# Weight-quarter sums by accumulating DMAs, token sums in six VectorE operations, output scaling on ScalarE, in an attention and top-1 expert kernel

## The chip, the cores and the metric

The kernel runs on one core of one Trainium2 chip. The metric is the device time in microseconds (us) of a whole execution. In the profile PE is TensorE, PEld its weight loads, DVE VectorE, ACT ScalarE, POOL GpSimd and SP SyncE; SPq and POOLq are the sequencers that issue DMAs.

## The reference

Attention with a linear bias over a window of 128 positions, then a layer of eight experts in which each token goes to one:

```python
x = attn_out.transpose(0, 2, 1, 3).reshape(4608, 512)     # attention, 8 x 8 heads, 576 positions
logits = xn @ en.T / tau
expert_idx = np.argmax(logits, axis=1)
gate_w = softmax(logits)[token, expert_idx]
for e in range(8):
    mask = expert_idx == e
    h = np.maximum(x[mask] @ w1[e], 0.0)                  # w1[e]: 512 x 1024
    out[mask] = gate_w[mask, None] * (h @ w2[e])          # w2[e]: 1024 x 512
```

All of it is float32. The kernel holds each factor as a high and a low float16 part and multiplies high by high, high by low and low by high.

## The kernel before

The first 300 us compute attention and the routing; tokens are scattered by expert into a DRAM buffer `xs`. The part that the change touches is `moe`, from about 270 us on. The experts are taken one after another as slots, each with a capacity in tokens (`SLOTS`, 512 to 688), in the order `TURNS` = 0, 1, 4, 3, 5, 6, 2, 7. Slots 0 and 1 (`PLAIN` = 2) use plain matmuls (`hidden`). The other six use a seven-product scheme for the first matmul: tokens are split into even and odd (halves of h columns, h = 256 to 312), the 512 inputs and the 1024 hidden units into halves, so that w1 has four quarters, named here 11, 12, 21, 22, and seven products of sums replace eight products of quarters (`seven`, the table `SEVEN`).

Stages of a slot s on PE: the **sevens** (four column groups `ft`, each seven steps of six matmuls, L1526), then the **output** (4 or 5 blocks of 128 tokens, 24 matmuls each with 512 columns, L1601; after slots 4 and 6 also one block `ps_t` that packs leftover tokens of several slots). While PE computes the output of one slot, the next slot is made ready:

- SP fetches w1 and w2 in pieces of 512 KB into a ring of `WSTG` = 6 staging tiles `ws` (`fetch`, L1397, L1399). A piece waits until the tile's former user is done.
- POOL makes the weight differences `tt`, `tu` from the w1 pieces (`differ`, L1431: eight per slot) and the token sums z1, z2, z4, z3 from the token tile `xT` (`x_sum`, L1451: ten per slot).
- ACT rounds every quarter, difference and sum to the high float16 part (L1414, L1461, for w2 L1483); DVE computes the low part from the same source and the high part (L1412, L1459, for w2 L1481). There is one pair of w1 part tiles, so these follow the sevens of the slot before.
- ACT or DVE in turn scales each output block by the gate (`scaled`, L1613, L1615) and POOL writes it to DRAM by token index (`put`, an indirect DMA, L440).
- DVE makes the row numbers `ids` and gates `gs` of the next slot (`row_info`, L1385 to L1388). These sit between the second and the third combining operation of the current slot's first column group; `ids` has two buffers, so the new one waits until the last `put` of the slot before the current one has landed.

In the sevens, ACT copies product a out of PSUM (`s`, L1539), DVE makes u2, u3 and the four quarters of the hidden layer from it (`combine`, L1537), ACT and DVE split these (`quarter`, L1559, L1557). Step 5 of a column group (ps7a again) waits for `s`, step 6 (ps7d) for u3, step 7 (ps7c) for the combining operation of ps7b.

A planner written in the kernel (`Plan.run`) sets the order: every operation is a job with an engine, an assumed duration, what it follows, what buffers it takes and a due time; each engine's instructions are then emitted in the order found. Engines work in order, so an instruction that waits holds up what is behind it.

Of the kernel before, what the change touches and what calls it, by code (L numbers as in the profile page):

```python
# [23 lines left out]
P = 128  # L24
# [12 lines left out]
WSTG = 6  # L37
# [164 lines left out]
def kernel(  # L202
# [1100 lines left out]
    def moe(mctx):  # L1303
        def pool(nm, n):
            return mctx.enter_context(tc.tile_pool(name=nm, bufs=n))

        xt, yp, st, ht, wT, wS, tp, zp = (
            pool(*a)
            for a in (("xt", 2), ("yp", 3), ("wstage", WSTG), ("ht", 1), ("wthird", 1), ("wseven", 1), ("wdiff", TBUFS), ("xsum", 1))
        )  # L1310
        MB = (MAXCAP + P - 1) // P
        MH = max(SLOTS[1:]) // 2
# [14 lines left out]
        def expert_of(s):  # L1327
            if s == 0:
                state[s] = dict(e=head_box["e"], w1=(w["w1h"], w["w1l"]), w2=(w["w2h"], w["w2l"]))
            else:  # L1330
                state[s] = dict(e=nc.sync.value_load(ebi[0:1, s : s + 1], min_val=0, max_val=E - 1))

# [71 lines left out]
        def split(s, what, c, lo):  # L1404

            if "w1" not in state[s]:
                state[s]["w1"] = [wS.tile([P, 2, 7, HF], F16, tag=f"w1{n}", name=f"w1{n}_{s}") for n in "hl"]
            i0, n = PIECES[what]
            x = {"a": ws[s, 1, c][:, 0:HF], "b": ws[s, 1, c + 2]}[what] if what in "ab" else ws[s, what, c].rearrange("p a f -> p (a f)")
            hi, lo_ = (a[:, c, i0 : i0 + n, :].rearrange("p a f -> p (a f)") for a in state[s]["w1"])  # L1410
            if lo:
                nc.vector.scalar_tensor_tensor(lo_, x, SW, hi, op0=ALU.mult, op1=ALU.subtract)  # L1412
            else:
                nc.scalar.activation(hi, x, AF.Copy, scale=SW)  # L1414

        def differ(s, i, c):

            what = "tu"[i // 2]
            if i % 2 == 0:
                ws[s, what, c] = tp.tile([P, 2, HF], F32, tag="tt", name=f"t{what}_{s}_{c}")  # L1420
            up, dn, o = ws[s, 1, c], ws[s, 1, c + 2], ws[s, what, c][:, i % 2, :]
            b11, b12, b21, b22 = up[:, 0:HF], up[:, HF:F], dn[:, 0:HF], dn[:, HF:F]
            if i == 0:
                a, b = b12, b11
            elif i == 1:
                a, b = b22, ws[s, "t", c][:, 0, :]
            elif i == 2:
                a, b = b22, b12
            else:
                a, b = b21, ws[s, "t", c][:, 1, :]  # L1430
            nc.gpsimd.tensor_tensor(o, a, b, op=ALU.subtract)  # L1431
# [3 lines left out]
        def x_sum(s, i, k):  # L1435

            h, xx = SLOTS[s] // 2, state[s]["xT"]
            a = {(t, d): [xx[:, b + 2 * d : b + 2 * d + 2, t : 2 * h : 2] for b in (0, KT)] for t in range(2) for d in range(2)}
            if k == 0:
                zs[s, i] = zp.tile([P, 2, MH], F32, tag="z", name=f"z{i}_{s}", bufs=ZBUFS)[:, :, 0:h]  # L1440
            z = zs[s, i]
            add, sub = ALU.add, ALU.subtract
            if i == 1:
                x, y, op = [(a[1, 0][0], a[1, 1][0], add), (z, a[1, 0][1], add), (z, a[1, 1][1], add)][k]
            elif i == 2:
                x, y, op = [(zs[s, 1], a[0, 0][0], sub), (z, a[0, 0][1], sub)][k]
            elif i == 3:
                x, y, op = [(a[0, 0][0], a[1, 0][0], sub), (z, a[0, 0][1], add), (z, a[1, 0][1], sub)][k]
            else:
                x, y, op = [(a[0, 1][0], zs[s, 2], sub), (z, a[0, 1][1], add)][k]  # L1450
            nc.gpsimd.tensor_tensor(z, x, y, op=op)  # L1451

        def x_split(s, i, lo):
            h = SLOTS[s] // 2
            if "S" not in state[s]:
                state[s]["S"] = zp.tile([P, 4, 2, 2, MH], F16, tag="S", name=f"S_{s}")
            hi, lo_ = (state[s]["S"][:, i - 1, b, :, 0:h] for b in range(2))
            if lo:
                nc.vector.tensor_tensor(lo_, zs[s, i], hi, op=ALU.subtract)  # L1459
            else:  # L1460
                nc.scalar.activation(hi, zs[s, i], AF.Copy)  # L1461

        def part(p, s, w, c, lo):
            if w == 1:
                if "w1" not in state[s]:
                    state[s]["w1"] = [
                        wS.tile([P, 2, 7, HF], F16, tag=f"w1{n}", name=f"w1{n}_{s}").rearrange("p a b f -> p (a b f)")[:, 0 : KT * F].rearrange("p (a f) -> p a f", f=F)
                        for n in "hl"
                    ]
# [42 lines left out]
        def seven(s, ft, n):  # L1512
# [12 lines left out]
            for m, (a, b, c) in enumerate(jobs):  # L1525
                nc.tensor.matmul(  # L1526
                    ps, a[:, c, idx, fs], b[:, c, :], start=(n in OPENS and m == 0), stop=(m == len(jobs) - 1), skip_group_check=True
# [6 lines left out]
        def combine(s, ft, what):  # L1534
            h = SLOTS[s] // 2
            b = {k: wb[s, ft, k][:, 0:h] for k in "abcd" if (s, ft, k) in wb}
            add = lambda o, x, y: nc.vector.tensor_tensor(o, x, y, op=ALU.add)  # L1537
            if what == "s1":
# [5 lines left out]
            elif what == "c22":  # L1544
                add(b["b"], b["c"], su[s, ft, "u3"])
            else:
                o = b["d" if what == "c21" else "c"]
                add(o, o, su[s, ft, "u2"])
# [77 lines left out]
        plan.caps.update(pt=8, ws=WSTG, xT=2, info=2, rows=2, h=1, y=3, w10=1, w1s=1, w20=1, w21=1, w22=1, tt=TBUFS, z=ZBUFS, S=1, s1=1, u2=2, u3=1)  # L1626
# [20 lines left out]
        for p, s in enumerate(TURNS):  # L1647
# [17 lines left out]
            if p:  # L1665
                last_ = TURNS[p - 1]
                m = starts[last_] + 24 * (0.42 * SLOTS[last_] + 5) * (3.5 if p > PLAIN else 4 if p > 1 else 2)
                for w_ in (1, 2):
                    for c in range(4):
                        d = (lead if w_ == 1 else m) + 1500 * c + 500  # L1670
                        a = (p, s, w_, c)
                        J(
                            f"get{w_}_{s}_{c}", "SP", 640, lambda a=a: fetch(*a), land=1800, moves=1400, makes=[("ws", ("ws",) + a)],
                            due=d - 3000 * (w_ == 1), after=before(f"expert{s}") + before(f"rows{last_}") + ([(f"get{w_}_{s}_{c-1}", ORDER)] if c else []),
                        )
                for c in range(2 if p >= PLAIN else 0):
                    up, dn = ("ws", p, s, 1, c), ("ws", p, s, 1, c + 2)
                    for i in range(4):
                        tk = ("tt", s, "tu"[i // 2], c)
                        J(  # L1680
                            f"dif_{s}_{c}_{i}", "POOL", 1130, lambda a=(s, i, c): differ(*a), lock=(1130,),
                            after=[f"get1_{s}_{c}", f"get1_{s}_{c + 2}"] + ([f"dif_{s}_{c}_{i - 1}"] if i else []),
                            makes=[("tt", tk)] if i % 2 == 0 else [], uses=[tk, up, dn] + ([("tt", s, "t", c)] if i == 3 else []), due=lead + 4000 + 5000 * c + 1200 * i,
                        )
                    for n, what in enumerate("btua"):
                        src = {"a": [up], "b": [dn], "t": [("tt", s, "t", c)], "u": [("tt", s, "u", c)]}[what]
                        dep = {"a": [f"get1_{s}_{c}"], "b": [f"get1_{s}_{c + 2}"], "t": [f"dif_{s}_{c}_1"], "u": [f"dif_{s}_{c}_3"]}[what]
                        half = what == "a"
# [249 lines left out]
```

## Time and profile before

| | us |
|---|---|
| median of 3 runs | 704.51 (701.58 to 704.75) |
| the profiled execution, its time | 699.6 |
| its span, first to last instruction | 697.9 |
| PE / DVE / ACT / POOL busy | 600.5 / 544.2 / 374.8 / 436.3 |

The span is 1.7 us under the profiled execution's own time, and that is 4.9 us under the median. Busy shares are means over the span; attention and the expert layer differ, so the views below are read by stretch. A row of a timeline gives start, duration, engine, line, operation, output<-input, and in brackets how long the engine had been idle and what released it.

### The profile page before, as it was taken

Reading aid. Unit: us, or ns where it says so; the run is one execution under the profiler, and the core shown is the slowest. Engines: PE = TensorE matmul, PEld = TensorE weight load, DVE = VectorE, ACT = ScalarE, POOL = GpSimd, SP = SyncE. Lnnn points to the kernel's source line nnn. Section 1 sums busy time; section 2 is a strip of 40 time slices with the busy share of each in tenths; the row PEclk is TensorE's granted clock in tenths of the full one; section 3 lists DMA queues with packets and bytes.
Section 4 is the critical chain, followed back from the end, with each engine's and each line's share of the span. In section 5 each row is a group of like instructions: output and inputs, shape, how many; then the busy total and the mean of one; then the engine's idle time right before and its main releaser. Section 6 shows DMA issues by size and latency. Waiting matters only on the chain. (4 is left out here: it accounts for less than half of the span.)

```text
span 697.9 us, 17376 instructions
## 1 busy us (share of the span) xinstructions
PE 600.5 (86%) x6613; PEld 402.7 (58%) x6613; DVE 544.2 (78%) x1203; ACT 374.8 (54%) x860; POOL 436.3 (63%) x563
## 2 busy tenths in 40 slices
PE   7999998999898899989939973992996797499996
PEld 5877777777766655556427442741744543264664
DVE  5987998999989991735926986796796798769680
ACT  6999897988879741622603622441461362235320
POOL 8878598789888872059680686098078368607301
PEclk9999999999999999999988995998899799599999
DMA  9999999999999777983630651173084055300101
GB/s 196 192 192 175 198 212 200 197 234 204 192 257 203 114 236 242 264 220 66 183 141 1 144 181 56 36 225 108 1 241 138 1 162 176 95 1 16 57 16 47
DMA packets 213589, 101.52 MB, mean 145 GB/s; under 512 B 195829, under 2 KB 195829, under 8 KB 213504
## 3 DMA queue, kind: packets, MB, share of 16 engines
q1 hardware_dynamic: 207664, 81.47, 56.6%
q0 software_dynamic: 5840, 18.92, 7.5%
q8 instruction: 53, 0.87, 0.5%
q14 instruction: 32, 0.26, 0.1%
HBM read 61.92 MB, written 19.70 MB: 117 GB/s over the span
## 5 line engine op out<-in xcount | busy, mean ns | idle before, releaser
L1526 PEld LDWEIGHTS <-w1h 128*128 128x128 f16 x672 | 68.6, 102 | 84.6 <-issue 63.9
L1601 PE MATMUL ps<-w2h,hl 128*128 128x512 f16 (+1 forms) x264 | 98.4, 373 | 0.6 <-DVE hl L1565 0.5
L1601 PE MATMUL ps<-w2h,hh 128*128 128x512 f16 (+1 forms) x264 | 98.4, 373 | 0.0
L1601 PE MATMUL ps<-w2l,hh 128*128 128x512 f16 (+1 forms) x264 | 98.4, 373 | 0.0
L688 ACT ACTIVATE pe<-sc,nm 128x128 f32<-128x128 f32 x288 | 85.0, 387 | 7.5 <-DVE rs L780 2.9
L1601 PEld LDWEIGHTS <-hh 128*128 128x128 f16 x528 | 51.5, 98 | 57.7 <-issue 0.8
L1451 POOL TENSOR_TENSOR z<-xT,z 128x528 f32<-128x528 f16 (+4 forms) x6 | 12.5, 2076 | 113.1 <-DVE S L1459 113.0
L440 POOL DMA_INDIRECT out_dram<-y,ids x32 | 41.8, 1306 | 56.6 <-DMA xs<-zrow 22.9
L1451 POOL TENSOR_TENSOR z<-z,xT 128x528 f32<-128x528 f32 (+4 forms) x42 | 70.3, 1675 | 2.1
L540 DVE SCALAR_TENSOR_TENSOR pq<-ptp,pq 128x512 f16<-128x512 f32 x72 | 53.0, 736 | 13.8 <-ACT pq L537 13.7
L1526 PE MATMUL ps7c<-S,w1h 128*128 128x264 f16 (+4 forms) x192 | 39.0, 297 | 25.9 <-DVE ps7b L1537 25.9
L537 ACT ACTIVATE pq<-ptp 128x512 f16<-128x512 f32 x72 | 55.2, 767 | 10.3 <-PE ptp L696 7.6
L1526 PE MATMUL ps7a<-xT,w1h 128*128 128x264 f16 (+4 forms) x192 | 40.9, 305 | 21.5 <-ACT s L1539 21.5
L1481 DVE SCALAR_TENSOR_TENSOR w2l<-ws,w2h 128x1024 f16<-128x1024 f32 x28 | 53.1, 1911 | 7.7 <-ACT w2h L1483 7.7
L696 PE MATMUL ptp<-ident,pe 128*128 128x128 f32 x288 | 48.0, 284 | 12.2 <-DVE pq L540 5.8
L1559 ACT ACTIVATE hh<-ps7b 128x264 f16<-128x264 f32 (+4 forms) x24 | 11.6, 484 | 86.8 <-DVE ps7b L1537 86.8
L664 PE MATMUL sc<-kh,qh 64*64 64x192 f32 (+3 forms) x1280 | 57.7, 288 | 0.0
L681 DVE TENSOR_REDUCE nm<-sc 128x2 f32<-128x256 f32 x144 | 55.7, 410 | 0.1
L664 PEld LDWEIGHTS sc<-kh,qh 64*64 64x64 f32 (+1 forms) x1280 | 44.6, 139 | 8.7 <-issue 3.5
L1483 ACT ACTIVATE w2h<-ws 128x1024 f16<-128x1024 f32 x28 | 28.8, 1050 | 37.6 <-DMA ws<-moe_w_dram 37.6
L813 POOL TENSOR_TENSOR gx<-xf,gx 128x512 f16<-128x512 f32 x36 | 42.2, 1173 | 8.5 <-DVE gx L802 6.0
L613 POOL TENSOR_TENSOR vo<-ldv,vh 128x512 f16<-128x512 f32 x36 | 40.7, 1135 | 6.7 <-ACT vh L605 6.2
(272 smaller groups left out, 1842.1 us busy)
## 6 DMA issues: line engine op xcount, KB each, us to landing
ws<-moe_w_dram SPq DMA_DIRECT2D x56, 512.0 KB, 4.8
ldk<-k_dram SPq DMA_DIRECT2D x32, 256.0 KB, 4.7
ldq<-q_dram SPq DMA_DIRECT2D x32, 256.0 KB, 4.9
ldv<-v_dram SPq DMA_DIRECT2D x32, 256.0 KB, 5.2
stg<-moe_w_dram SPq DMA_DIRECT2D x16, 256.0 KB, 4.0
ldk<-k_dram SPq DMA_DIRECT2D x8, 128.0 KB
ldq<-q_dram SPq DMA_DIRECT2D x8, 128.0 KB, 4.7
ldv<-v_dram SPq DMA_DIRECT2D x8, 128.0 KB, 5.3
```

What stands on the lines that cost most here:

```text
L440: ins = nc.gpsimd.indirect_dma_start(out[:, :], bass.IndirectOffsetOnAxis(ap=ids, axis=0), y, None, bounds_check=NTOK - 1, oob_is_err=False)
L537: nc.scalar.activation(hi, ps, AF.Copy, scale=scale)
L540: nc.vector.scalar_tensor_tensor(lo, ps, scale, hi, op0=ALU.mult, op1=ALU.subtract)
L664: nc.tensor.matmul(sc[T, hf, j][o, l, c], qT[T]["h"][rows, hp, o], x["h"][rows, hp, c.start + at : c.stop + at], start=False, stop=True, s ...
L681: nc.vector.tensor_reduce(nm_t[T, hf, j], sc[T, hf, j][:, :, 0:P], axis=AX.X, op=ALU.min)
L688: nc.scalar.activation(pr_t[T, hf][:, 2 * l + j, :], ps[:, l, 0:P], AF.Exp, bias=nm[:, l : l + 1], scale=-1.0)
L696: nc.tensor.transpose(pt[:, i, :], pe[:, i, :], ident)
L813: nc.gpsimd.tensor_tensor(xx[:, DM : 2 * DM], xf_t[T], xx[:, 0:DM], op=ALU.subtract)
L1451: nc.gpsimd.tensor_tensor(z, x, y, op=op)
L1481: nc.vector.scalar_tensor_tensor(lo_, x, SW, hi, op0=ALU.mult, op1=ALU.subtract)
L1526: nc.tensor.matmul(ps, a[:, c, idx, fs], b[:, c, :], start=(n in OPENS and m == 0), stop=(m == len(jobs) - 1), skip_group_check=True)
L1601: nc.tensor.matmul(ps, x[:, ft, a * P : (a + 1) * P], w[:, ft, c], start=(n == 0), stop=(n == len(jobs) - 1))
```

## The change

The sign of two weight quarters is turned in the scheme, so that all four weight combinations are sums of quarters and none is a difference: t1 = 12+11, t3 = 22+12, t2 = t3+11, t4 = t2+21. SP fetches five quarters (512 KB each: 11, 22, 21, and the start values of t1 and t3), and POOL issues four DMAs that read a quarter from DRAM and add it to a staging tile (`gather`). t2 and t4 are formed in t3's tile, so each waits until DVE has taken the low part of the sum before. The signs go into the rounding operations' scale and into `combine` (`neg`). `differ` and its tiles are gone.

The token sums are made on DVE: two operations `rebuild` add the high and low parts of all four token quarters into one tile z, and four `x_sum` form z1, z3, z2, z4 in place. They replace ten operations on POOL. The outputs are scaled on ACT, but for slots 0 and 1 and half of the last block. The staging ring has 8 tiles, and the part tiles of w1 hold the products outermost.

```diff
-WSTG = 6
+WSTG = 8
-PIECES = {"a": (0, 1), "b": (1, 2), "t": (3, 2), "u": (5, 2)}
+XSUM = "DVE"
+PIECES = {
+    "11": (0, (0, 0), 1),
...
+CHAINS = {"t1": [(0, 0)], "t3": [(0, 1)], "t2": [(0, 0)], "t4": [(1, 0)]}
+WIDTHS = {"t2": (4, -1), "t4": (6, 1)}
...
+        def fetch_quarter(s, what):
+            ws[s, what] = x = st.tile([P, 2, HF], F32, tag="ws", name=f"ws_{what}_{s}")
+            nc.sync.dma_start(x, quarter_of(s, PIECES[what][1], state[s]["e"]))
+
+        def gather(s, what, q):
+
+            if what in ("t2", "t4"):
+                ws[s, what] = ws[s, "t3"]
+            nc.gpsimd.dma_start(ws[s, what], quarter_of(s, q, state[s]["ep"]), accum_op=ALU.add)
...
-            nc.gpsimd.tensor_tensor(o, a, b, op=ALU.subtract)
...
+        def rebuild(s, d):
             h, xx = SLOTS[s] // 2, state[s]["xT"]
...
+            x, y = (xx[:, b + 2 * d : b + 2 * d + 2, 0 : 2 * h].rearrange("p k (j t) -> p k t j", t=2) for b in (0, KT))
+            (nc.gpsimd if XSUM == "POOL" else nc.vector).tensor_tensor(zs[s][:, d, :, :, 0:h], x, y, op=ALU.add)
+
+        def x_sum(s, i):
+
+            s1, s2, s3, s4 = (z_of(s, k) for k in (1, 2, 3, 4))
+            o, x, y = {1: (s1, s3, s1), 3: (s3, s2, s3), 2: (s2, s2, s1), 4: (s4, s2, s4)}[i]
+            (nc.gpsimd if XSUM == "POOL" else nc.vector).tensor_tensor(o, x, y, op=ALU.subtract)
...
+            neg = lambda o, x, y: nc.vector.scalar_tensor_tensor(o, x, -1.0, y, op0=ALU.mult, op1=ALU.subtract)
...
-                add(b["b"], b["c"], su[s, ft, "u3"])
+                neg(b["b"], b["c"], su[s, ft, "u3"])
...
+                    dep = {"t1": "getq_{}_t1", "t3": "getq_{}_t3", "t2": "slo_{}_t3", "t4": "slo_{}_t2"}
...
-                    e = ("ACT", "DVE")[(n_out + i) % 2]
+                    e = ("ACT", "DVE")[(n_out + i) % 2 if p < PLAIN or two else 0]
```

What this does to the order is shown at two places. The first is DVE in the output of slot 3, where slot 5 is made ready. Names end in the slot and a running number: `ws1_5_2` is piece 2 of w1 of slot 5, `ws_t3_5` and `ws_11_5` are quarter tiles of slot 5, `z1_5` a token sum. Before:

```order
L1459 TENSOR_TENSOR S_5_8973<-z2_5_8615,S_5_8973 128x2x264
L1615 TENSOR_SCALAR y_3_0_9026<-ps2_3_0_0_8944,gs_3_8104 128x512
L1412 SCALAR_TENSOR_TENSOR w1l_5_8941<-ws1_5_0_8557,w1h_5_8940 128x512
L1412 SCALAR_TENSOR_TENSOR w1l_5_8941<-ws1_5_3_8574,w1h_5_8940 128x1024
L1412 SCALAR_TENSOR_TENSOR w1l_5_8941<-tt_5_1_8659,w1h_5_8940 128x1024
L1412 SCALAR_TENSOR_TENSOR w1l_5_8941<-tu_5_1_8985,w1h_5_8940 128x1024
L1459 TENSOR_TENSOR S_5_8973<-z4_5_8980,S_5_8973 128x2x264
L1412 SCALAR_TENSOR_TENSOR w1l_5_8941<-ws1_5_1_8561,w1h_5_8940 128x512
L1481 SCALAR_TENSOR_TENSOR w2l_5_8648<-ws2_5_2_9044,w2h_5_8647 128x1024
L1459 TENSOR_TENSOR S_5_8973<-z3_5_9048,S_5_8973 128x2x264
```

The same place after; `z_9062` is the sum tile of the slot after, slot 6:

```order
L1435 SCALAR_TENSOR_TENSOR w1l_5_8952<-ws_t1_5_8618,w1h_5_8951 128x1024
L1435 SCALAR_TENSOR_TENSOR w1l_5_8952<-ws_11_5_8655,w1h_5_8951 128x1024
L1465 TENSOR_TENSOR S_5_8984<-z_5_8535,S_5_8984 128x2x264 x2
L1435 SCALAR_TENSOR_TENSOR w1l_5_8952<-ws_21_5_8649,w1h_5_8951 128x1024
L1465 TENSOR_TENSOR S_5_8984<-z_5_8535,S_5_8984 128x2x264
L1435 SCALAR_TENSOR_TENSOR w1l_5_8952<-ws_22_5_8647,w1h_5_8951 128x1024
L1451 TENSOR_TENSOR z_6_9062<-xT_6_8942 128x4x264
L1435 SCALAR_TENSOR_TENSOR w1l_5_8952<-ws_t3_5_8616,w1h_5_8951 128x1024
L1451 TENSOR_TENSOR z_6_9062<-xT_6_8942 128x4x264
L1457 TENSOR_TENSOR z_6_9062<-z_6_9062 128x2x264 x4
L1435 SCALAR_TENSOR_TENSOR w1l_5_8952<-ws_t3_5_8616,w1h_5_8951 128x1024
```

The two last w1l rows are t2 and t4, each behind an accumulating DMA; the token sums stand on DVE one slot early, and the output scaling and the w2l rows have left this stretch.

The second place is POOL in the output of slot 4, where slot 3 starts next and slot 5 is being fetched. Before, differences of slot 5 stand between the puts:

```order
L1431 TENSOR_TENSOR tt_5_0_8617<-ws1_5_0_8557 128x512
L1431 TENSOR_TENSOR tt_5_0_8617<-ws1_5_2_8571,tt_5_0_8617 128x512
L440 DMA out_0_dram<-y_4_2_8645,ids_4_7548 4608x512
L1431 TENSOR_TENSOR tu_5_0_8654<-ws1_5_2_8571,ws1_5_0_8557 128x512
L1431 TENSOR_TENSOR tu_5_0_8654<-ws1_5_2_8571,tt_5_0_8617 128x512
L1431 TENSOR_TENSOR tt_5_1_8659<-ws1_5_1_8561 128x512
L440 DMA out_0_dram<-y_4_3_8668,ids_4_7548 4608x512
```

After, accumulating DMAs do: t4 of slot 3 ahead of three puts, and the first sums t3 and t1 of slot 5 ahead of the last put of slot 4:

```order
L1425 DMA ws_t3_3_8053<-moe_w1_dram 128x2x512
L447 DMA out_0_dram<-y_4_t_8565,ids2_0_7210 4608x512
L447 DMA out_0_dram<-y_4_1_8579,ids_4_7531 4608x512
L447 DMA out_0_dram<-y_4_2_8645,ids_4_7531 4608x512
L1425 ISA
L1425 DMA ws_t3_5_8616<-moe_w1_dram 128x2x512
L1425 ISA
L1425 DMA ws_t1_5_8618<-moe_w1_dram 128x2x512
L447 DMA out_0_dram<-y_4_3_8674,ids_4_7531 4608x512
```

But for a few memsets no arithmetic is left on POOL in this part; what it waits for now is SP's fetches and DVE's w1l rows.

## Rows read from the trace of the kernel before

**Rows 1.** The page's first part: busy us, share of the span, instructions.

```profile
PE 600.5 (86%) x6613; PEld 402.7 (58%) x6613; DVE 544.2 (78%) x1203; ACT 374.8 (54%) x860; POOL 436.3 (63%) x563
```

**Rows 2.** Stretches of 20 us: length, engines' busy us, granted clock, DMA share, GB/s.

```profile
370.00:390.00 20.00, 20.00 (x142) 14.29 (x141) 14.17 (x31) 9.66 (x20) 0.33 (x1) 0.92 0.21 46
...
410.00:430.00 20.00, 6.44 (x39) 3.92 (x38) 14.29 (x10) 3.49 (x5) 19.22 (x14) 0.69 0.45 152
430.00:450.00 20.00, 18.25 (x137) 13.73 (x137) 14.86 (x38) 6.75 (x16) 0.57 (x1) 0.89 0.00 1
...
490.00:510.00 20.00, 20.00 (x150) 14.91 (x149) 16.28 (x39) 10.40 (x22) 0.03 (x1) 0.94 0.18 33
...
610.00:630.00 20.00, 20.00 (x134) 13.24 (x133) 13.58 (x28) 8.57 (x18) 0.00 (x0) 0.95 0.00 1
```

**Rows 3.** Waits of the whole span: who waited for whom, us, times, longest.

```profile
PE ps7c L1526 <- DVE ps7b L1537: 25.9, 3, 11.7
...
PE ps7a L1526 <- ACT s L1539: 21.5, 3, 8.0
...
PE ps7d L1526 <- DVE u L1537: 14.2, 4, 8.3
...
PE ps7d L1526 <- DVE S L1459: 3.9, 2, 2.1
```

**Rows 4.** Timelines of DVE, POOL and ACT at the waits' sources.

```profile
359.34 1.28 POOL L1431 TENSOR_TENSOR tu<-ws,tt 128x512 f32<-128x512 f32 x1
...
363.33 0.99 POOL L440 DMA_INDIRECT out_dram<-y,ids  x1 [0.15 <-issue]
366.20 0.16 DVE L1387 SCALAR_TENSOR_TENSOR ids<-got,far 128x4 int32<-128x4 f32 x1 [10.42 <-DMA out_dram<-y,ids]
```

**Rows 5.** ACT and DVE later, before PE's waits for `s` and u.

```profile
417.03 1.06 ACT L1483 ACTIVATE w2h<-ws 128x1024 f16<-128x1024 f32 x1 [8.71 <-DMA ws<-moe_w_dram]
...
422.56 4.34 DVE L1385 CAST got<-info 128x4 f32<-128x4 int32 x1
```

**Rows 6.** DVE and POOL timelines: DVE beside POOL arithmetic, beside a put, alone.

```profile
397.56 3.98 DVE L1412 SCALAR_TENSOR_TENSOR w1l<-tt,w1h 128x1024 f16<-128x1024 f32 x1
...
406.94 2.34 DVE L1481 SCALAR_TENSOR_TENSOR w2l<-ws,w2h 128x1024 f16<-128x1024 f32 x2
407.30 1.72 POOL L440 DMA_INDIRECT out_dram<-y_t,ids  x1 [2.16 <-DVE y_t L1615]
...
453.51 0.70 DVE L1459 TENSOR_TENSOR S<-z,S 128x528 f16<-128x528 f32 x1
454.13 1.22 DVE L1412 SCALAR_TENSOR_TENSOR w1l<-tt,w1h 128x1024 f16<-128x1024 f32 x1
```

**Rows 7.** Groups from 300 us on: busy us, mean ns, idle before.

```profile
L1451 POOL TENSOR_TENSOR z<-z,xT 128x528 f32<-128x528 f32 (+4 forms) x42 | 70.3, 1675 | 2.1
...
L1481 DVE SCALAR_TENSOR_TENSOR w2l<-ws,w2h 128x1024 f16<-128x1024 f32 x24 | 48.3, 2027 | 7.4 <-ACT w2h L1483 7.4
...
L1613 ACT ACTIVATE y<-ps,gs 128x512 f32<-128x512 f32 (+1 forms) x15 | 9.9, 660 | 21.2 <-PE ps L1601 18.6 <-DMA out_dram<-y,ids 2.6
```

**Rows 8.** PE's timeline where slot 3's sevens end and its output begins.

```profile
449.51 0.41 PE L1526 MATMUL ps7c<-S,w1h 128*128 128x288 f16 x2
...
450.24 0.38 PE L1601 MATMUL ps<-w2h,hh 128*128 128x512 f16 x1
450.45 0.38 PE L1601 MATMUL ps<-w2l,hh 128*128 128x512 f16 x1
```

**Rows 9.** The put's tile view: ns min/median/max on POOL; landing from issue.

```profile
L440 POOL DMA_INDIRECT out_dram<-y,ids x32: 967/1259/1992, 295.9 to 693.8; - x32
...
DMA to landing us min/median/max: 2.7/5.2/9.4
```

**Rows 10.** The tile view of `ws` from 300 us on: landing from issue.

```profile
DMA to landing us min/median/max: 3.7/4.2/6.5
```

**Rows 11.** The page's third part: POOL's DMA queue, packets, MB, share of 16 engines.

```profile
q0 software_dynamic: 5840, 18.92, 7.5%
```

More of the change, by code (lines that the diff above doesn't have):

```diff
@@ L1406, in split @@
+        def split(s, what, lo):
             if "w1" not in state[s]:
[L1407 to L1410, printed above, removed]
+                state[s]["w1"] = [wS.tile([P, 7, 2, HF], F16, tag=f"w1{n}", name=f"w1{n}_{s}") for n in "hl"]
+            at, sign = WIDTHS[what] if what in WIDTHS else PIECES[what][::2]
+            x = ws[s, what].rearrange("p a f -> p (a f)")
+            hi, lo_ = (a[:, at].rearrange("p a f -> p (a f)") for a in state[s]["w1"])
@@ L1411, in split @@
             if lo:
-                nc.vector.scalar_tensor_tensor(lo_, x, SW, hi, op0=ALU.mult, op1=ALU.subtract)
+                nc.vector.scalar_tensor_tensor(lo_, x, sign * SW, hi, op0=ALU.mult, op1=ALU.subtract)
             else:
[L1414 to L1430, printed above, removed]
-            nc.gpsimd.tensor_tensor(o, a, b, op=ALU.subtract)
+                nc.scalar.activation(hi, x, AF.Copy, scale=sign * SW)
@@ L1433, in moe, with z_of @@
         zs = {}
-        def x_sum(s, i, k):
+        def z_of(s, i):
+            t, d = ((1, 1), (0, 0), (1, 0), (0, 1))[i - 1]
+            return zs[s][:, d, :, t, 0 : SLOTS[s] // 2]
+        def rebuild(s, d):
             h, xx = SLOTS[s] // 2, state[s]["xT"]
[L1438 to L1451, printed above, removed]
+            if s not in zs:
+                zs[s] = zp.tile([P, 2, 2, 2, MH], F32, tag="z", name=f"z_{s}")
+            x, y = (xx[:, b + 2 * d : b + 2 * d + 2, 0 : 2 * h].rearrange("p k (j t) -> p k t j", t=2) for b in (0, KT))
+            (nc.gpsimd if XSUM == "POOL" else nc.vector).tensor_tensor(zs[s][:, d, :, :, 0:h], x, y, op=ALU.add)
@@ L1526, in seven @@
                 nc.tensor.matmul(
-                    ps, a[:, c, idx, fs], b[:, c, :], start=(n in OPENS and m == 0), stop=(m == len(jobs) - 1), skip_group_check=True
+                    ps, a[:, idx, c, fs], b[:, c, :], start=(n in OPENS and m == 0), stop=(m == len(jobs) - 1), skip_group_check=True
                 )
@@ new lines, in moe @@
+                sp_last = None
+                seven_ = p >= PLAIN
+                first_gets = [("q", what) for what in ("t3", "t1", "22", "21", "11")] if seven_ else [(1, c) for c in range(4)]
+                for n, (w_, c) in enumerate(first_gets + [(2, c) for c in range(4)]):
+                    d = (lead - 3000 if w_ != 2 else m) + 1500 * n
+                    if w_ == "q":
+                        name, key, emit = f"getq_{s}_{c}", ("ws", s, c), lambda a=(s, c): fetch_quarter(*a)
+                    else:
+                        name, key, emit = f"get{w_}_{s}_{c}", ("ws", p, s, w_, c), lambda a=(p, s, w_, c): fetch(*a)
+                    J(
+                        name, "SP", 640, emit, land=1800, moves=1400, makes=[("ws", key)], due=d,
+                        after=before(f"expert{s}") + before(f"rows{last_}") + (before(sp_last) if sp_last else []),
+                    )
+                    sp_last = name
```

112 lines of the change are left out of this document (55 added, 57 removed).

## The prediction

> **What bounds the kernel now.** I read the page's busy shares first, then stretches of 20 us, then PE's waits and what stood behind each. PE is busy 86% of the span [rows 1], so no engine is simply full; the question is where PE stands still. The stretches answer: from 300 us on, full ones alternate with one like 410 to 430, where PE has 6.4 us of work, DVE 14.3 and POOL 19.2 [rows 2]. These are the five starts of slots 4, 3, 5, 6 and 2. PE's waits there fall into four groups, 12 waits: 25.9 + 21.5 + 14.2 + 3.9 = **65.5 us** [rows 3]. The clock adds to it: a long wait is followed by a stretch in which the granted clock is 0.92, 0.89, 0.94, 0.95 [rows 2], since PE starts at the lower of its two levels, 1.2 GHz, and reaches 2.4 GHz some us later: 20 x (0.08 + 0.11 + 0.06 + 0.05) = **6.0 us**. The span without both is 697.9 - 65.5 - 6.0 = 626.4 us.
>
> Behind the waits stands POOL, in three ways. (1) A put comes late since differences are queued ahead of it; DVE's `ids` waited 10.4 us for a put to land, with the operation that PE's step 7 needs behind it [rows 4]. (2) POOL's arithmetic slows DVE: a w1l row that takes 1.22 us alone took 3.98 beside POOL's sums [rows 6], and the 24 w2l rows have a mean of 2.03 [rows 7]. That frees staging tiles late: ACT waited 8.7 us for a w2 piece with `s` behind it, and a cast of four columns took 4.3 us on DVE with u behind it [rows 5]. (3) The token sums themselves come late.
>
> **The change part by part.**
>
> *POOL's arithmetic goes.* 42 of the 60 sums alone are 70.3 us [rows 7]; all 60 and the 48 differences leave POOL. The mechanisms (1) to (3) lose their cause, and the 65.5 and 6.0 us with them, as far as nothing takes their place.
>
> *DVE gets six operations per slot.* Two of about 1,090 columns at twice 0.70 us and four of 530 at 0.70 [rows 6]: 5.6 us per slot, 34 in all. Nearest rows for the bounds: 0.70 alone for 528 columns, and, should something still slow them, three times that, as 3.98 to 1.22 [rows 6]. They cost nothing on the path if they are covered by PE's output stage. DVE's work there, in the output of slot 3: seven w1l x 1.22 = 8.5, four S x 0.70 = 2.8, the new six 5.6, together 16.9 us. PE's output is four blocks of 24 matmuls that follow at 0.21 us [rows 8], 4 x 5.2 = 20.7 us. So the cover holds by 4 us. After slots 4 and 6 three w2l rows (3.7) lie there as well, and a packed block (5 us) with them. Were the cover gone, 3.98 in place of 1.22 for each w1l alone would add 19 us to a stage.
>
> *Scaling moves to ACT*: some 13 blocks x 0.66 us [rows 7]; ACT is busy 54% [rows 1] and in the stretch 430 to 450 a third, so I cost it at nothing. The sign operations are as long as the additions they replace; also nothing.
>
> *Row numbers still wait for a put.* That is late next. After PE's last block of a slot: 0.2 to be seen, y 0.66 [rows 7], 0.2, a put that lands after 2.9 (363.33 to 366.20, [rows 4]) up to the median 5.2 [rows 9]; I take 4.0, as POOL is emptier; then ids and its neighbours 0.8 and the combining operation 0.5: 6.4 us. PE reaches step 7 after six steps of 0.73 [rows 8] = 4.4. A wait of 2.0 (0.9 to 3.2), at three slots (4, 5, 6). At slots 3 and 2 the last put stands behind two accumulating DMAs of the slot after on POOL, which themselves wait for SP's fetches: 2 x 1.26 [rows 9] more, 4.5 us. Together 3 x 2.0 + 2 x 4.5 = **15 us** (9 to 21).
>
> *The accumulating DMAs.* The trace has none; call L the time from POOL's start of one to its sum being seen by ACT. From below: a plain fetch of the same 512 KB, 4.2 us [rows 10]. From above: the slowest put, 9.4 [rows 9], plus two more passes of the bytes: POOL's queue moved 18.92 MB in 7.5% of 16 engines' 697.9 us [rows 11], so 0.52 MB take 1.45 us, and 9.4 + 2.9 = 12.3. I take 4.2, with POOL's 1.26 in place of SP's 0.4, plus one more pass: **6.5 us**, nearer the fetch, which is the same transfer but for the adding.
>
> Where does L show? The chain in the output of slot 3, from its first matmul: the first w1l, t3's, ends where S begins now, at 453.51 - 450.24 = 3.3 [rows 6, 8]; t2 is seen at 3.4 + L, 9.9; DVE comes to it after four more w1l, four S and one rebuild, 3.3 + 4.9 + 2.8 + 1.4 = 12.4, done 13.6; POOL has put y1 out by then, t4 is seen at 20.2 and, after ACT's 1.1 and DVE's 1.2, done at 22.5. PE wants t4 at step 6: 20.7 + 5 x 0.73 = 24.4. So 6.5 fits with 2 us to spare. But t3's tile is also that of the last w2 piece, and behind that piece stand on SP the next slot's five quarters, the first w2 piece of that slot, and so an ACT row in the sevens: 22.5 + 4.2 and more. Hence a few us at one or two slots: **4 us** (0 to 12). Beyond about 6.5 each further us is met twice per slot, at t2 and t4, for six slots: 12 us per us of L.
>
> DMA traffic rises by nine pieces in place of four for w1 per slot, 2.6 MB; DMA is busy 0.00 to 0.45 of the time in the stretches of [rows 2], so I cost it in L alone.
>
> The Trainium skill, page "DMA: Bandwidth & Descriptors", section "Anatomy of one DMA - SWDGE (gpsimd) path", fits a DMA issued by GpSimd as 2.0 us + bytes / 436e3: 3.2 us for 512 KB, an estimate. By it the 4 us term would be 0 and the forecast 648. The rows stand against it: puts of half the size take 2.7 to 9.4.
>
> Sum: 697.9 - 65.5 - 6.0 + 15 + 4 = 645.4 us of span. The profiled execution's own time is 1.7 over its span and the median of the runs 4.9 over that: 652.0, say **652 us**.
>
> **The rivals.**
>
> *Slow sums.* L of 7.5 to 10.5, since the DMA engines read a destination, add and write it back while SP's stream of pieces shares them. For it: the put's range up to 9.4. Against: the engines are idle half of the time. At 9.5: 652 - 4 + 12 x 3 = 684.
>
> *Starved issue.* The Trainium skill, page "SBUF - State Buffer", section "Summary: rules for kernel authors", says that descriptor generation on GpSimd is starved while VectorE is in a fast mode, and advises issuing from ACT or SP; an accumulating DMA can't be. What the trace shows: beside w2l rows at full speed (2.34 for two) a put took 1.72 us [rows 6], without them 0.99 [rows 4]; the put stretches by 0.7, and DVE isn't slowed. Were the issue blocked for a whole DVE row instead, 1.2 us, L would be 7.7 and the time 652 - 4 + 12 x 1.2 = 662.
>
> *Not what it says.* DVE stays slow, because POOL's DMA issue slows it as its arithmetic did. Then seven w1l at 2.03 instead of 1.22 add 5.7, and S and sums half as much again, 4: 26.6 against 20.7, 6 us at six slots, 652 + 36 = 688. The 2.34 for two w2l beside a put speaks against it [rows 6].
>
> *Slower.* The chain of accumulating DMAs becomes the bound: t2 must be split before t4 can be added. From L = 6.5 + (704.5 - 648) / 12 = 11.2 on, the change loses; at 12.3, the upper bound, 648 + 12 x 5.8 = 718. For it: three passes over the bytes and no row of the kind. Against: it needs the slowest put's wait each time.
>
> **How the numbers follow.** Forecast 0.60 (some 640 to 668, from the put term at 9 with the chain at 0, to 21 and 12), slow sums 0.17, starved issue 0.07, DVE stays slow 0.04, slower 0.12 (a tenth for the upper bound, and some for things not seen). The range: 640 to 695, which leaves out the slower case and little below. A measurement of this kernel tells about 0.5% from no change, 3.5 us. Faster by more: 0.60 + 0.16 + 0.07 + 0.03 = 0.86; within: 0.03, from slow sums near L = 11; slower 0.11.
>
> **What would show it.** Right: w2l and w1l rows near 1.2 us wherever they stand, casts of `got` near 0.15; PE's waits from 300 us on below 25 us in sum, with `ids <- DMA out` as the first source and largest at slots 3 and 2; granted clock near 1.00 in all stretches. L can be read from the start of POOL's DMA on `ws` to the ACT row on it. Wrong: ACT or DVE rows on `ws` waiting several us for a DMA at each slot, with PE's wait on `s` or u behind them; DVE's w1l rows still at 2 us; or POOL's DMA rows on `ws` themselves of several us.

## The result and the profile after

The changed kernel takes 675.98 us (median; 673.03 to 678.1) where the kernel before, on the same chip, takes 703.05: ratio **0.9635**, 95% interval 0.9587 to 0.9683 (the two medians alone give 0.9615). The profiled execution took 673.03 us, its span 671.3. The forecast was 652, a gain of 52 us; 27 came. Direction and range held, half of the gain did not come.

The page's busy times and DMA queues, against [rows 1] and [rows 11]:

```profile
PE 604.5 (90%) x6613; PEld 405.5 (60%) x6613; DVE 481.7 (72%) x1220; ACT 381.1 (57%) x867; POOL 308.8 (46%) x479
...
q1 hardware_dynamic: 212368, 84.62, 58.7%
q0 software_dynamic: 12368, 31.50, 18.7%
```

POOL lost 128 us of work and DVE 62. But PE is busy 4 us longer than before with the same 6613 matmuls, and the software queue fills the 16 engines for 18.7% of the span in place of 7.5%. The added 24 transfers took (0.187 x 671.3 - 0.075 x 697.9) / 24 = 3.05 us of all engines each, about twice the 1.45 of a plain pass.

VectorE's groups from 300 us on (busy us, mean ns, idle before them), against [rows 7]:

```profile
L1487 DVE SCALAR_TENSOR_TENSOR w2l<-ws,w2h 128x1024 f16<-128x1024 f32 x26 | 31.3, 1218 | 8.9 <-ACT w2h L1489 8.9
L1435 DVE SCALAR_TENSOR_TENSOR w1l<-ws_t,w1h 128x1024 f16<-128x1024 f32 x24 | 29.3, 1222 | 39.9 <-ACT w1h L1437 39.9
...
L1457 DVE TENSOR_TENSOR z<-z 128x528 f32<-128x528 f32 (+4 forms) x24 | 17.5, 731 | 0.6
...
L1451 DVE TENSOR_TENSOR z<-xT 128x1056 f32<-128x1056 f16 (+4 forms) x12 | 15.5, 1300 | 0.4 <-DMA xT<-xs 0.4
```

Each of these groups is at its undisturbed length, and the new token sums take 33.0 us (34 were forecast). What did not come out is in the waits from 300 us on (us in sum, times, longest), against [rows 3]:

```profile
ACT w1h L1437 <- DMA ws_t<-moe_w_dram: 53.0, 10, 12.7
...
PE ps7c L1532 <- DVE ps7b L1544: 26.5, 5, 10.7
DVE ids L1397 <- DMA out_dram<-y,ids: 20.7, 3, 10.7
...
PE ps7a L1532 <- ACT s L1546: 8.2, 2, 4.1
```

PE's waits in the sevens are 26.5 + 8.2 + 0.4 (u) = 35.1 us: 30 less than before, where 46 less were forecast. All of these 30 us come from the waits on `s`, u and S; the group behind `ids`, the first line for PE, has not shrunk at all (25.9 before). The longest is at the change from slot 4 to slot 3. POOL's, ACT's and DVE's timelines there; the first row is t4's accumulating DMA, the ACT row the one that reads its sum:

```profile
394.80 1.23 POOL L1425 DMA_DIRECT2D ws_t<-moe_w_dram  x1 [4.58 <-DVE w1l L1435]
...
405.21 1.06 ACT L1437 ACTIVATE w1h<-ws_t 128x1024 f16<-128x1024 f32 x1 [6.95 <-DMA ws_t<-moe_w_dram]
...
407.12 1.27 POOL L447 DMA_INDIRECT out_dram<-y,ids  x1 [6.78 <-ACT y L1621]
408.36 2.63 POOL L1425 DMA_DIRECT2D ws_t<-moe_w_dram  x2
411.30 1.08 POOL L447 DMA_INDIRECT out_dram<-y,ids  x1 [0.30 <-issue]
...
421.71 0.17 DVE L1397 SCALAR_TENSOR_TENSOR ids<-got,far 128x4 int32<-128x4 f32 x1 [10.72 <-DMA out_dram<-y,ids]
```

Stretches of 6 us around it (length; busy us of PE, PEld, DVE, ACT, POOL; granted clock; DMA share; GB/s):

```profile
402.00:408.00 6.00, 6.00 (x31) 2.76 (x30) 1.40 (x2) 2.60 (x4) 0.88 (x1) 1.00 1.06 361
408.00:414.00 6.00, 4.39 (x36) 3.27 (x34) 2.34 (x5) 1.57 (x3) 4.08 (x4) 1.00 1.06 380
414.00:420.00 6.00, 0.00 (x0) 0.00 (x0) 0.00 (x0) 0.00 (x0) 0.00 (x0) 0.73 1.06 228
```

The last put stands behind two accumulating DMAs (2.63 us), is issued at 411.30 and lands at 421.7, 10.4 us later. From about 412.4 on every compute engine stands still, and the DMA engines are full until about 420. They are full since SP, freed at 394.9, issues between 394.9 and 409.5 the last piece of w2, five quarters of the slot after and its first three w2 pieces. Hardly any of it is wanted so soon: ACT reads that piece of w2 at 406.7, the next ones at 426.8 and the first of the five quarters at 442.4.

### The profile page after: what moved, and what is told of

It reads as the page before. It is cut to its first block, busy times and chain, and to the rows that moved or that the text cites. A ratio compares the mean times of both kernels' runs of the same rounds, so it can differ in the third digit from the quotient of the medians.

```text
span 671.3 us, 17414 instructions
## 1 busy us (share of the span) xinstructions
PE 604.5 (90%) x6613; PEld 405.5 (60%) x6613; DVE 481.7 (72%) x1220; ACT 381.1 (57%) x867; POOL 308.8 (46%) x479
## 3 DMA queue, kind: packets, MB, share of 16 engines
q0 software_dynamic: 12368, 31.50, 18.7%
## 5 line engine op out<-in xcount | busy, mean ns | idle before, releaser
L1425 POOL DMA_DIRECT2D ws_t<-moe_w_dram x24 | 30.8, 1392 | 197.6 <-DVE w1l L1435 176.5
L447 POOL DMA_INDIRECT out_dram<-y,ids x32 | 53.5, 1670 | 86.6 <-ACT y L1621 58.7
L1532 PE MATMUL ps7c<-S,w1h 128*128 128x264 f16 (+4 forms) x192 | 39.1, 298 | 26.5 <-DVE ps7b L1544 26.5
L703 PE MATMUL ptp<-ident,pe 128*128 128x128 f32 x288 | 48.0, 284 | 13.1 <-DVE pq L547 5.5
L1435 DVE SCALAR_TENSOR_TENSOR w1l<-ws_t,w1h 128x1024 f16<-128x1024 f32 x24 | 29.3, 1222 | 39.9 <-ACT w1h L1437 39.9
L1437 ACT ACTIVATE w1h<-ws_t 128x1024 f16<-128x1024 f32 x24 | 25.1, 1049 | 53.0 <-DMA ws_t<-moe_w_dram 53.0
L1512 PE MATMUL ps<-xT,w1h 128*128 128x288 f16 (+2 forms) x192 | 42.7, 317 | 4.8 <-DVE hl L1573 2.8
L703 PEld LDWEIGHTS ptp<-ident,pe 128*128 128x128 f32 x288 | 31.6, 141 | 23.4 <-ACT pe L695 13.8
```

The costliest lines, as they stand in the source:

```text
L447: ins = nc.gpsimd.indirect_dma_start(out[:, :], bass.IndirectOffsetOnAxis(ap=ids, axis=0), y, None, bounds_check=NTOK - 1, oob_is_err=False)
L703: nc.tensor.transpose(pt[:, i, :], pe[:, i, :], ident)
L1425: nc.gpsimd.dma_start(ws[s, what], quarter_of(s, q, state[s]["ep"]), accum_op=ALU.add)
L1512: nc.tensor.matmul(ps[:, :w], a[:, kt, fs], xx[:, b + kt, c0 : c0 + w], start=(n == 0), stop=(n == len(jobs) - 1))
L1532: nc.tensor.matmul(ps, a[:, idx, c, fs], b[:, c, :], start=(n in OPENS and m == 0), stop=(m == len(jobs) - 1), skip_group_check=True)
```

## The experiments

The diffs are shortened; `...`, angle brackets and words in round brackets stand for what is left out. Ratios are to the kernel before, measured beside each run. Theory A: puts and t4 land late because pieces and accumulating DMAs crowd the DMA engines and the queue. Theory B: a put's landing is seen only because the row numbers have two buffers. Rival C: the addition itself is slow. The prediction's own reading was that GpSimd's arithmetic stands behind the waits of before. "Behind `ids`" stands for PE's waits on the operation that follows the row numbers (ps7c on ps7b); to land is to be seen by the row that waits.

**Three buffers for the row numbers.**

```diff
-            ids = yp.tile([P, MB], I32, tag="ids", name=f"ids_{s}", bufs=2)
+            ids = yp.tile([P, MB], I32, tag="ids", name=f"ids_{s}", bufs=3)
     (the same for gs; the planner's rows=2 becomes 3)
```

> The changed kernel with three buffers in place of two for the row numbers and the scales of a slot, so that a slot's row numbers no longer wait for the last put of the slot two before. Theory A (crowded transfers: at a slot change the pieces of the slot after, the accumulating DMAs and the puts fill the DMA engines, so puts and t4 land late) and theory B (the two buffers alone make a put's landing visible) both expect that PE's waits on the combining operation behind ids, 26.5 us in sum, go, and 8 to 9 us of waits on s stay: 676 - 26.5 = 649, with half-clock time partly given back 642 to 652. Rival C (something else is late right behind, t4 or the pieces of w2, so that PE's wait only changes its name): 662 to 676.

Measured: 641.12 us, ratio 0.9077 (0.905 to 0.9104). That is just under the 642 to 652 of both theories; that another wait takes the place falls. PE's waits from 300 us on:

```profile
PE ps7a L1532 <- ACT s L1546: 5.7, 2, 3.1
PE ps L1512 <- DVE hl L1573: 4.4, 1, 4.4
PE ps7d L1532 <- DVE u L1543: 0.4, 1, 0.4
```

The waits behind `ids` are gone, those on `s` stay (5.7), and the granted clock's mean rises from 0.960 to 0.991. The span, 636.1 us, is below the 645.4 that the prediction's sum gave.

**The fetches held back.**

```diff
-            nc.sync.dma_start(x, quarter_of(...))
+            d = nc.sync.dma_start(x, quarter_of(...))
+            if what == "t3":
+                sync_dep(d, state[TURNS[TURNS.index(s) - 2]]["put"])
     (the put is kept in `state`; the planner lets this fetch wait for it as well)
```

> The changed kernel, but the fetch of a slot's first quarter waits until the last put of the slot two before has landed; the four other quarters and three pieces of w2 stand behind it on SP. The same bytes, moved out of the output stage into the sevens, where DMA was busy 0.01 to 0.55. Theory A: the last puts land in 3 to 5 us in place of up to 10, t4 is seen 5 to 7 us after its issue in place of up to 10.8; PE's waits of 35.1 us from 300 us on fall to 12 to 20, the time to 652 to 664. Theory B: the landing costs the wait by itself, crowded or not; waits stay over 25 us, 668 to 676. Theory C (the adding itself takes 6 to 10 us): t4's time and the waits on s stay, 664 to 676. Slower than 680 if the pieces now come too late for the next output stage.

Measured: 641.89 us, 0.9062 (0.9036 to 0.9087), better than A's range; PE's waits from 300 us on fall to 13.2. The put and the row numbers at the same place in this kernel:

```profile
406.80 0.98 POOL L447 DMA_INDIRECT out_dram<-y,ids  x1 [4.20 <-ACT y L1623]
...
409.76 0.16 DVE L1397 SCALAR_TENSOR_TENSOR ids<-got,far 128x4 int32<-128x4 f32 x1 [1.74 <-DMA out_dram<-y,ids]
```

The stretches there:

```profile
402.00:408.00 6.00, 6.00 (x38) 3.48 (x37) 1.87 (x4) 1.39 (x3) 1.59 (x2) 1.00 0.13 46
408.00:414.00 6.00, 4.41 (x36) 3.28 (x35) 3.84 (x15) 2.21 (x5) 0.00 (x0) 1.00 0.59 196
414.00:420.00 6.00, 6.00 (x50) 4.69 (x49) 4.75 (x11) 2.11 (x6) 2.54 (x2) 1.00 1.00 312
```

The put lands 2.9 us after its issue, since DMA is busy 0.13 then; the bytes move a little later, beside a PE that works. t4 is seen 5.9 us after its issue (392.61 to 398.55) where it took 10.4 (394.80 to 405.21). B's claim that the landing costs the wait crowded or not falls: two buffers nearly do when the put lands quickly (3.4 us of waits behind `ids` are left).

**The transfer without the addition.**

```diff
-            nc.gpsimd.dma_start(ws[s, what], quarter_of(...), accum_op=ALU.add)
+            nc.gpsimd.dma_start(ws[s, what], quarter_of(...))
```

> The changed kernel with the addition left out of the 24 accumulating DMAs: the same transfers, at the same places, that overwrite their tile instead of adding (so the weight sums are wrong). Measures what the adding costs. Theory A: the software queue's share of the engines falls from 18.7% to about 13%, since one of two passes goes; landing falls from a median of 6.7 us to 5 to 6, less where the engines are full; waits on s go from 8.2 to 3 us or less; 662 to 670. Theory C (adding is slow in itself): landing falls to 3.5 to 4.5 everywhere, 655 to 664. If the plain pieces of SP alone crowd the engines, landing and time stay: 672 to 678.

Measured: 666.14 us, 0.9427 (0.9388 to 0.9466). The software queue's share is 13.1%, 1.44 us of all engines for each transfer, so the addition doubles a transfer's use of the engines, and its issue takes POOL 0.78 us in place of 1.34. At the same place t4 took 7.5 us (395.98 to 403.51) and the waits behind `ids` fall from 26.5 to 18.2: the addition is a part of the crowd, some 2 points of ratio, not the whole of it. Theory C falls as the sole cause, since an addition took 5.9 us where the engines were free. The waits on `s` stay at 6.8 where 3 or less were expected.

**The weight sums as GpSimd arithmetic.**

```diff
-            nc.gpsimd.dma_start(ws[s, what], quarter_of(...), accum_op=ALU.add)
+            nc.gpsimd.tensor_tensor(ws[s, what], ws[s, what], ws[s, ADDEND[what]], op=ALU.add)
```

> One part undone: the four sums of quarters per slot are made by GpSimd arithmetic on the fetched tiles (128 x 1024 columns, from the 1.67 us for some 550 columns in the kernel before about 3.2 us each, 77 us in all) and no accumulating DMA is left; the token sums stay on VectorE and the scaling on ScalarE. If the gain came from freeing VectorE of GpSimd's arithmetic: w1l, w2l and S rows go back towards 2 us, 685 to 700. If the token sums were the larger part and the accumulating DMAs cost as much as they bring: 660 to 676, with the DMA engines' software queue back near 7.5% and puts landing earlier.

Measured: 661.04 us, 0.9357 (0.9327 to 0.9386): faster than the changed kernel. DVE's rows on weights are slow again (group: busy us, mean ns, idle before):

```profile
L1440 DVE SCALAR_TENSOR_TENSOR w1l<-ws_t,w1h 128x1024 f16<-128x1024 f32 x24 | 40.0, 1670 | 4.7 <-ACT w1h L1442 4.6
```

But PE's waits in the sevens are only 23.7 us:

```profile
PE ps7d L1537 <- DVE u L1548: 19.6, 4, 6.4
PE ps7c L1537 <- DVE ps7b L1549: 4.1, 1, 4.1
```

But for one wait of 4.1 us the puts land in time, with nothing but puts in POOL's DMA queue. So with two buffers the accumulating DMAs cost 2.8 points more than additions on GpSimd.

**Three buffers in the kernel before.** The edit of the first run, nothing of the change.

> The kernel before with three buffers in place of two for row numbers and scales, nothing of the change. Theory B alone (two buffers are what PE waits for, in both kernels): PE's 25.9 us of waits on the combining operation go and some half-clock time with them, ratio to the kernel before 0.95 to 0.965. The prediction's own reading (GpSimd's arithmetic is the cause; the put is one of three ways in which it shows, and s and u are late right behind): ratio 0.98 to 1.0, the waits on s and u grow from 21.5 and 14.2 us.

Measured: 670.62 us, 0.9431 (0.9386 to 0.9477): more than the whole change gained, and better than B's range. PE's waits from 300 us on, the longest:

```profile
PE ps7a L1526 <- ACT s L1539: 16.0, 2, 8.9
PE ps7d L1526 <- DVE u L1537: 8.7, 3, 4.0
PE ps7a L1526 <- DVE w1l L1412: 4.3, 2, 2.2
```

The 25.9 us behind `ids` [rows 3] go, and the other waits do not grow to fill the place; only the 4.3 us on w1l are new. That GpSimd's arithmetic was by itself the cause of this, the largest, group falls: with all of it in place the group goes. The arithmetic may still have made the puts late there (differences stand ahead of the put in [rows 4]); what the run shows is that a late put costs only with two buffers. With three buffers in both kernels the change is worth 0.9077 / 0.9431 = 0.9625, about what it is worth with two.

**The token sums back on GpSimd.**

```diff
-XSUM = "DVE"
+XSUM = "POOL"
```

> One part undone: the six token sums per slot back on GpSimd (1.67 us for 528 columns in the kernel before, so about 2 x 3.3 + 4 x 1.67 = 13 us per slot, 80 us in all); accumulating DMAs and scaling stay. If the move to VectorE earned much of the gain: w1l and S rows beside the sums 2 to 4 us, puts and accumulating DMAs queued behind sums, ratio to the kernel before 0.985 to 1.01. If it earned little: 0.955 to 0.975, as the changed kernel's 0.9635.

Measured: 698.15 us, 0.983 (0.9797 to 0.9864). That is a little below the 0.985 to 1.01 expected for a move that earned much. The sums cost POOL 70.5 us, w1l on `ws_t` has a mean of 1482 ns, and PE waits 23.1 us on u and 17.2 behind `ids`. The move to VectorE earned 2 of the change's 3.65 points.

**The scaling in turn again.**

```diff
-                    e = ("ACT", "DVE")[(n_out + i) % 2 if p < PLAIN or two else 0]
+                    e = ("ACT", "DVE")[(n_out + i) % 2]
```

> One part undone: outputs scaled in turn by ScalarE and VectorE. The prediction costed the move at nothing: ratio 0.957 to 0.970, as the changed kernel's 0.9635. Rival: since ScalarE's y now stands behind its row on t4, which waits up to 10 us for the accumulating DMA, the move delays the last puts; undoing it gives ratio 0.940 to 0.955 with shorter waits behind ids. A loss (over 0.975) would say that VectorE has no room for six or seven rows of 0.7 us per slot.

Measured: 0.9657 (0.9624 to 0.9691), as forecast no difference that can be told.

**Three buffers and held fetches together.** Both edits from above.

> Three buffers for row numbers and scales together with the first quarter's fetch held until the last put two slots before has landed. If both take away the same wait (theories A and B are the two halves of one cause): within 1% of either alone, ratio 0.897 to 0.910, with what is left of the waits on s and u. If each also takes away waits of its own: 0.885 to 0.897. Slower than either (over 0.912) if holding delays t3 of the next slot where nothing was waiting.

Measured: 643.39 us, 0.9064 (0.9032 to 0.9095): as either alone. A and B are the two halves of one cause; taking away either half takes away the wait, or nearly so.

**Accumulating DMAs behind the last put.**

```diff
-                            after=[f"epool{s}", dep[what].format(s)],
+                            after=[f"epool{s}", dep[what].format(s)] + ([] if late else before(<the last put, two slots before>)),
```

> The changed kernel with one order changed on GpSimd: the first two accumulating DMAs of the slot after (t3, t1) stand behind the last put of a slot, not ahead of it; SP's fetches stay where they were. The prediction's own step (the put issued late because two accumulating DMAs stand ahead of it, 2.5 us at two slots, is what makes those waits larger): 4 to 7 us less, ratio 0.953 to 0.959, waits behind ids 26.5 down to 18 to 22. Theory A (the landing is long because SP's pieces fill the engines, whatever the order on GpSimd): ratio 0.959 to 0.967, the last put at slot 3's change still lands 8 us or more after its issue. If the two accumulating DMAs were the crowd: as the kernel that holds the fetches, 0.91 to 0.93.

Measured: 667.96 us, 0.9433 (0.9372 to 0.9494), better than the prediction's step and theory A gave, and short of the 0.91 to 0.93 of the third reading (these two DMAs are the crowd). Waits behind `ids` fall from 26.5 to 11.4 us, though u (7.1) appears. The put at slot 3's change, in the timelines:

```profile
414.94 0.98 POOL L447 DMA_INDIRECT out_dram<-y,ids  x1 [0.94 <-ACT y L1621]
415.90 2.63 POOL L1425 DMA_DIRECT2D ws_t<-moe_w_dram  x2
...
421.06 0.16 DVE L1397 SCALAR_TENSOR_TENSOR ids<-got,far 128x4 int32<-128x4 f32 x1 [4.90 <-DMA out_dram<-y,ids]
```

And the stretch around its landing:

```profile
414.00:420.00 6.00, 3.62 (x30) 2.70 (x28) 1.33 (x4) 1.57 (x3) 3.60 (x4) 1.00 1.05 396
```

SP's pieces still fill the engines (1.05), yet the put lands 6.1 us after its issue in place of 10.4. It is issued 14.2 us after SP's burst begins (at 400.70 here), the other one 16.5 us after (394.85), so it does not meet the burst later. Of the 7.5 us above the quiet 2.9, then, 4.3 went with the two accumulating DMAs ahead of it, and 3.2 are left, beside SP's pieces.

**Which way to add, once nothing waits for puts.** Three buffers, with the sums on GpSimd; with t2 and t4 on VectorE; with all four on VectorE (the edit as above, with `nc.vector` in place of `nc.gpsimd`):

> Three buffers for row numbers and scales, and the sums of quarters made by GpSimd arithmetic as in the run that undid this part. With two buffers that undoing gained 2.8 points of ratio. If the accumulating DMAs lost only because they lengthen the puts' landing, which two buffers expose, they win here: the waits on u that GpSimd's arithmetic leaves (19.6 us) stay, ratio 0.920 to 0.935 against 0.908 with accumulating DMAs. If accumulating DMAs are the worse choice in themselves: 0.880 to 0.905.

> Three buffers, and t2 and t4 made on VectorE from the fetched quarters (two additions of 1024 columns, 1.2 us each by the S and z rows, per slot) in place of the two chained accumulating DMAs; t1 and t3 stay accumulating DMAs. If what is left with three buffers is the chain t3, t2, t4 (waits on s of 5.7 us, ScalarE up to 13.3 us on a DMA) the waits on s go: ratio 0.893 to 0.904. If VectorE has no room for 2.4 us more in an output stage (some 17 of 20.7 us taken): waits on u and the combining operation, 0.912 to 0.925. If nothing of it is on the path any more: 0.904 to 0.911.

> Three buffers, and all four sums of quarters per slot on VectorE (four additions of 1024 columns, some 1.2 us each); no accumulating DMA is left, and the software queue falls back to about 7.8% of the engines. Says whether the two accumulating DMAs that the run before kept (t1 and t3, off the chain) still earn anything. If they are free where nothing waits for them and VectorE fills up: ratio 0.895 to 0.910, with waits on u or the combining operation. If their transfers still crowd the puts and pieces: 0.880 to 0.890. Within 0.889 to 0.895: no difference.

Measured: 647.8 us, 0.9115 (0.9072 to 0.9159); 632.35 us, 0.8921 (0.8873 to 0.897); **616.63 us, 0.8823** (0.879 to 0.8856). With accumulating DMAs and three buffers it was 0.9077. GpSimd's additions and the DMAs are now equal within the intervals, both of my expectations for that run missed; VectorE's additions beat them, and the last kernel beats both kernels of this study. Which part of the last step (0.8921 to 0.8823) is due to the two transfers is not shown: in neither run does PE wait in the sevens, and the run that kept them has PE busy 594.3 us against 585.9, with half-clock stretches from 154 and 318 us that the last kernel has not. Of the last kernel's 24 additions on DVE, 18 form this group:

```profile
L1430 DVE TENSOR_TENSOR ws_t<-ws_t,ws 128x1024 f32<-128x1024 f32 x18 | 21.9, 1218 | 0.0
```

All of PE's waits from 268 us on, then two stretches of 40 us:

```profile
PE ps L1517 <- DVE hl L1578: 1.6, 1, 1.6
PE ps L1517 <- DMA xT<-xs: 1.3, 1, 1.3
PE ps L1614 <- DVE hl L1578: 0.2, 1, 0.2
```

```profile
380.00:420.00 40.00, 40.00 (x258) 24.87 (x256) 36.40 (x60) 21.19 (x36) 4.22 (x4) 1.00 0.48 149
420.00:460.00 40.00, 40.00 (x266) 25.73 (x265) 38.20 (x71) 23.05 (x40) 8.01 (x6) 1.00 0.56 176
```

PE is never held in the sevens, its clock is granted in full, and DVE has 36 to 38 us of work in 40.

## Why the prediction was right in part, step by step

- **POOL's arithmetic goes, DVE runs free, sums are covered, scaling and signs cost nothing**: right, by the rows above and the run that put the scaling back. That DVE's cover held by 4 us per stage was even cautious: four more rows per slot fit.
- **Row numbers wait for a put**: the mechanism and its place were right (first source, largest at slots 3 and 2: 10.7 and 5.2 us), the size was not: 26.5 us where the term was 15 (9 to 21). The step that failed most is "2 x 1.26 [rows 9] more": it priced the issue of the two accumulating DMAs on POOL and not their transfer, which the put's landing follows. At slot 3 they cost 2.6 + 4.3 us, not 2.5, and 3.2 more went beside SP's pieces. At slots 4, 5 and 6, where none stands ahead, the waits were 3.5, 3.9 and 3.2 us and not 2.0, as the puts landed in 4.3 to 5.5 us where 4.0 was taken, "as POOL is emptier": the crowd is not on POOL.
- **DMA traffic, "I cost it in L alone"**: wrong. I had read DMA's share of 0.00 to 0.45 in the stretches of [rows 2], where PE waits and little is fetched; in the full ones beside them, which I left out, it was 0.52 to 0.73 after 390 us. The traffic comes in bursts at the slot changes, at a share of 1.06, just when the puts must land.
- **The accumulating DMAs**: L = 6.5 was a fair middle (landing 5.8 / 6.8 / 10.8 us, least, median, most; 5.9 seen where the engines are free, 10.4 in the crowd), but the term that hangs on it, 4 us, came out at 8.6 (8.2 on `s`, 0.4 on u). The story of the last w2 piece waiting for t3's tile did not happen: SP fetched that piece at 394.9, before t4 was split at 406.3. It is a w2 piece of the slot after that waited: SP issued it at 407.55, just as t4's low part ended, and no wait of PE follows from it. What happened is that ACT, working in order, stood at t4's row with y and `s` behind it.
- **The clock, 6.0 us to be won back**: wrong twice. The loss before was larger: PE was busy 27.46 us in the stretches at 1.2 GHz and so lost half of that, 13.7 us; I had counted only four of the stretches that followed waits. And it did not go: after the change it is 32.16 / 2 = 16.1 us, in seven stretches, five at the slot changes and two behind waits of 2.0 and 2.8 us ahead of them. PE's busy time tells it in one line: 604.5 against 600.5 us, 4.0 more, of which these stretches give 2.4. The half-clock stretches (length, PE's busy us, granted clock, DMA share, GB/s), one row and the sum, of the kernel before:

```profile
359.40:373.10 13.70, 5.84 (x26) 0.50 0.10 39
...
sum 71.70, PE 27.46; mean PE 5.49
```

And after:

```profile
467.60:481.20 13.60, 8.28 (x38) 0.51 0.70 160
...
sum 51.00, PE 32.16; mean PE 4.59
```

The terms close the account. Against the forecast span of 645.4 us: put term +11.5, chain +4.6, and PE's busy time +4.0 where -6.0 was forecast, +10.0; together 26.1, and the span is 25.9 longer. (As a span is PE's busy time and its waits, such a sum has to come near; it says where the 26 us lie.) The last kernel checks the floor: with 13.7 in place of 6.0 it is 697.9 - 65.5 - 13.7 = 618.7 us, and with no wait left in the sevens its span is 614.8 and PE's busy time 585.9, 14.6 under that of before.

Of the rivals, "DVE stays slow" and "slower" fell, and "slow sums" came half true, through the puts rather than through L. Long issues, as "starved issue" has them, are there at a few places and longer than priced; their cause is open (below). That the stated range held is in part luck: 676 lies outside the 640 to 668 of the forecast itself, and the room above was there for rivals on L and on VectorE, not for the puts. A reading was loose, too: the w1l row of 1.22 us at 454.13 was not alone, since a sum on POOL starts at 454.35; another, at 452.37, was, and took 1.23.

The deeper miss is that the prediction named the put's landing as late next and did not ask what a third buffer would do, in either kernel. That run on the kernel before (0.9431) shows that the largest wait goes without taking any of that work away, and the changed kernel, with accumulating DMAs in its place, has the wait as large as it was.

## What to carry to other kernels

Where a wait is for a DMA to land, count what stands ahead of it in its queue and what else fills the engines at that moment, by short stretches around the wait, not by the mean; then ask whether one more buffer takes the wait away, before the work ahead of it is moved. An addition handed to a DMA is not free: it takes the engines' time twice, here at the slot changes where they were full, while VectorE had room for it. In the changed kernel, where the waits were fewer and shorter, the stretches at the lower clock stayed; in the last kernel, where the waits are gone, so are they.

## What was not expected of the hardware

- An accumulating DMA of 512 KB took 3.05 us of all 16 engines, the same transfer without the addition 1.44; it landed in 5.8 to 10.8 us. The Trainium skill's fit ("DMA: Bandwidth & Descriptors", section "Anatomy of one DMA - SWDGE (gpsimd) path") gives 3.2 us as an estimate; even where the engines were free 5.9 passed.
- GpSimd's issue of a put, 1.1 us in the median, took 9.89, 4.58 and 3.40 us at three places. VectorE was busy for 17.5 of these 17.9 us. The first, and VectorE's rows at its end:

```profile
500.94 9.89 POOL L447 DMA_INDIRECT out_dram<-y,ids  x1 [1.61 <-ACT y L1621]
...
508.41 1.45 DVE L1451 TENSOR_TENSOR z<-xT 128x1248 f32<-128x1248 f16 x1
509.90 3.34 DVE L1457 TENSOR_TENSOR z<-z 128x624 f32<-128x624 f32 x4
```

DVE's rows overlap up to 509.86, where the first break of 0.04 us comes, and the put ends 0.97 us after it. At 608.27 the same: a break at 610.70, the end at 611.67; at 449.24 no break is to be seen. t4's accumulating DMA of slot 6 stood behind the first, and PE's wait of 4.14 us on `s` followed. The Trainium skill ("SBUF — State Buffer", section "Summary: rules for kernel authors") says that descriptor generation on GpSimd is starved while VectorE is in a fast mode. No run here shows that VectorE was in one: its rows beside the long issue take some 1.2 ns a column (1.45 us for 1248), as its rows of 1024 columns do everywhere else (1.22). And a put at 389.13 took 1.09 us beside an equally unbroken VectorE, so the condition is not known from these runs; no run was made on it. The kernel that is fastest has such rows as well (up to 6.53 us), and with three buffers no wait of PE in the sevens follows from them.
